# Attention's inner loop regrouped: tiles of four heads by 256 queries, three at a time

## The chip, the cores and the metric

The kernel runs on one core of a Trainium2 chip. The core has a matrix engine (TensorE, PE in the profile), a vector engine (VectorE, DVE), an activation engine (ScalarE, ACT), GpSimd (POOL) and SyncE (SP), which issues transfers. Matmuls write into PSUM, eight banks of 512 fp32 columns on each of 128 partitions; the other engines read from there. Each engine works through its own list of instructions in order and waits on semaphores. The metric is the device time of one execution in microseconds: the median over the runs of a kernel.

## The reference

Four layers, each added to its input after a layer norm: a long convolution (a state space model applied by FFT), an attention, the same convolution, the same attention. The change touches only the attentions. 2048 positions, width 640, 32 heads of 20 queries each; keys and values are shared by all heads.

```python
def _B_ref(x, wq, wk, wv, wo):
    B, S, D = x.shape          # 1, 2048, 640
    H = 32
    Dh = D // H                # 20
    q = (x @ wq).reshape(B, S, H, Dh).transpose(0, 2, 1, 3)
    k = x @ wk
    v = x @ wv
    scores = jnp.einsum("bhqd,bkd->bhqk", q, k) * (Dh ** -0.5)
    p = _softmax(scores, axis=-1)
    o = jnp.einsum("bhqk,bkd->bhqd", p, v)
    return o.transpose(0, 2, 1, 3).reshape(B, S, H * Dh) @ wo

x = A_u
x = x + _A_ref(_layernorm(x), ...)
x = x + _B_ref(_layernorm(x), ...)    # layer "b"
x = x + _A_ref(_layernorm(x), ...)
x = x + _B_ref(_layernorm(x), ...)    # layer "d"
return x
```

## The kernel before

`tile_layers` runs kgen, convolution "a", attention "b", convolution "c", attention "d". In an attention, `_attn` first projects queries and keys; queries go to DRAM, split into a high and a low part of fp32 (`qhd`, `qld`), the keys stay in `kt`, the values in `vt` (32 columns, of which one is all ones, so that the sums of the softmax come out beside the values). Then `main_loop` does the work that the change rewrites.

The loop's unit is a *step* (nb, hg, t): a block of 512 queries nb (four of them), a *head group* hg of four heads (eight of them), and 128 keys t (sixteen). A step has two halves, pr = 0 and 1, two heads each:

- `scores(step, pr)`: a *score pair*, two matmuls side by side on PE (62 rows each: 20 + 20 + 20 for the split of the query and key, and two for an offset), one for each head of the half, into a PSUM tile `sc` of 128 x 1024 (two banks; there are three such tiles, `ps2`), and one exponential on ACT from `sc` to the SBUF tile `pt`.
- `values(step)`: for each of the four heads one fp32 matmul of 512 columns into 32 partitions of the bank `po`, which sums over the sixteen t. The hardware runs an fp32 matmul as two passes, each with its own weight load; the four heads run side by side.
- `projection(nb, t)`: at t = 2, 5, 8, 11 and 13 one *product* out of a queue, if there is one: a piece of the output projection (128 queries x 320 columns, 128 rows of `wo`), four matmuls of 320 columns into the bank `py`; `add` then adds it to x on VectorE.
- `normalize(nb, hg)` after t = 15: VectorE copies `po` out, takes the reciprocal and multiplies; SP's queue moves the result into `ot`, which later products read.

The order on PE and ACT is that of the code (`manual_schedule`); for the other engines a scheduler places instructions. In the code, step s + 2's first half of scores comes ahead of step s's values, and its second half behind them and behind a product. `po` always lies in PSUM bank 0 of the two single ones (`ps1`), `py` in bank 1. So a new head group's first values wait until VectorE has copied the old sums out. A score pair waits until the exponential three pairs earlier has read its PSUM tile.

`load_q` brings a head group's queries from DRAM: two tiles `qp` of 128 x 512, one per half, 16 transfers in all, into six such buffers.

Of the kernel before, what the change touches and what calls it, by code (L numbers as in the profile page):

```python
# [21 lines left out]
P = 128  # L22
# [13 lines left out]
SCALE = 20.0**-0.5  # L36
# [159 lines left out]
class Net:  # L196
# [873 lines left out]
    def load_q(self, pool, nm, nb, hg):  # L1070

        nc = self.nc
        cols = slice(512 * nb, 512 * nb + 512)
        for pr in range(2):
            q = pool.tile([P, 512], F32R, tag="qp", bufs=6, name=f"qp{nm}{nb}{hg}{pr}")
            h = 4 * hg + 2 * pr
            for par in range(2):
                rows = slice(20 * (h + par), 20 * (h + par) + 20)
                for r, src in ((2, self.qhd), (22, self.qhd), (42, self.qld)):
                    nc.sync.dma_start(q[64 * par + r : 64 * par + r + 20].bitcast(F32), src[rows, cols])  # L1080
                nc.sync.dma_start(q[64 * par : 64 * par + 2].bitcast(F32), self.mxd[h + par, :, cols])  # L1081
            self.qps[nb, hg, pr] = q

    def _attn(self, ctx, nm, out):
        tc, nc, ins = self.tc, self.nc, self.ins
        ap = ctx.enter_context(tc.tile_pool(name=f"at{nm}", bufs=1, reuse_waits="tile"))
        kt = ap.tile([P, L], F32R, name="kt")
        vt = ap.tile([P, 16, 32], F32, name="vt")
# [153 lines left out]
        with tc.If(fv == 0):  # L1242
            self.row_max(kt, nm)
            for pr in range(2):
                for par in range(2):
                    nc.sync.dma_start(self.qps[0, 0, pr][64 * par : 64 * par + 2].bitcast(F32),
                                      self.mxd[2 * pr + par, :, 0:512])

        k0, k64 = keys(512, 3)
        nc.vector.tensor_scalar(k0, ones_(0, 3), off[0:1], None, ALU.mult)  # L1250
# [2 lines left out]
        mp = ctx.enter_context(tc.tile_pool(name=f"mn{nm}", bufs=1, reuse_waits="tile"))  # L1253
        self.main_loop(ap, mp, kt, vt, nm, out)

    def main_loop(self, ap, mp, kt, vt, nm, out):
# [10 lines left out]
        tc, nc, qps = self.tc, self.nc, self.qps  # L1267
        wo = mp.tile([P, 5, D], F32, name="wo")
# [4 lines left out]
        def late_loads(late):  # L1273
            nc.gpsimd.memset(wol, 0.0)
            for j in range(4):
                nc.gpsimd.dma_start(wol[32 * j : 32 * j + 20],
                                    self.ins["B_wo"][20 * (28 + j) : 20 * (29 + j)])
            if out is None:
                self.conv_weights(nc.gpsimd, late)
# [5 lines left out]
        def scores(step, pr):  # L1285
            nb, hg, t = step
            if t == 0 and pr == 0:
                if (nb, hg, 0) not in qps:
                    self.load_q(ap, nm, nb, hg)
            sc = self.ps2(f"sc{nm}{nb}{hg}{t}{pr}")  # L1290
            for par in range(2):
                rows = slice(64 * par, 64 * par + 62)
                nc.tensor.matmul(sc[:, 512 * par : 512 * par + 512],  # L1293
                                 kt[rows, 128 * t : 128 * t + 128], qps[nb, hg, pr][rows],
                                 start=True, stop=True)
            pt = mp.tile([P, 1024], F32, tag="pt", bufs=6, name=f"pt{nb}{hg}{t}{pr}")
            nc.scalar.activation(pt, sc, AF.Exp, scale=SCALE)  # L1297
            pts[step, pr] = pt

        def values(step):  # L1300
            nb, hg, t = step
            if t == 0:
                pos[nb, hg] = self.ps1(f"po{nm}{nb}{hg}", 0)
            po = pos[nb, hg]

            for j in (2, 3, 0, 1):
                nc.tensor.matmul(po[32 * j : 32 * j + 32], vt[:, t],  # L1307
                                 pts[step, j // 2][:, 512 * (j % 2) : 512 * (j % 2) + 512],
                                 start=(t == 0), stop=(t == 15))
            for pr in range(2):  # L1310
                del pts[step, pr]

        def chunk(nb, k):
            if (nb, k) not in ots:
                ots[nb, k] = mp.tile([P, 512], F32, tag=f"ot{k}", bufs=2, name=f"ot{nb}{k}")
                if (nb, k) == (3, 4):

                    nc.gpsimd.memset(ots[nb, k], 0.0)
            return ots[nb, k]

        def normalize(nb, hg):
            po = pos.pop((nb, hg))
            on = mp.tile([P, 512], F32, tag="on", bufs=2, name=f"on{nb}{hg}")
            nc.vector.tensor_copy(on, po)  # L1324
# [12 lines left out]
            for k in range(80 * hg // 128, 80 * (hg + 1) // 128):  # L1337
                later.extend((nb, k, u) for u in range(8))
# [25 lines left out]
        def product(py, o, w, u, m, start, stop):  # L1364
            i, half = u // 2, u % 2
            for j in range(0, P, m):
                nc.tensor.matmul(py[j : j + m], o[:, 128 * i + j : 128 * i + j + m],  # L1367
                                 w[:, 320 * half : 320 * half + 320], start=start, stop=stop)

        def projection(b, t):  # L1370

            if t == (8 if b < 3 else 5):
                queue.extend(later)
                later.clear()
            if t in (2, 5, 8, 11, 13) and queue:
                nb, k, u = queue.pop(0)
                py = self.ps1(f"py{nm}{nb}{k}{u}", 1)[:, 0:320]
                product(py, ots[nb, k], wo[:, k], u, 32, True, True)
                add(nb, u, py, k == 4)

        with tc.manual_schedule(engines={mybir.EngineType.PE, mybir.EngineType.Activation}):
            for step in steps[:2]:
                for pr in range(2):
                    scores(step, pr)
            for s, step in enumerate(steps):
                nb, hg, t = step
# [8 lines left out]
                if (nb, hg, t) == (0, 1, 0):  # L1395
                    late_loads(pts[steps[s + 2], 0])
# [8 lines left out]
            last.append(self.ps1(f"pl{nm}6", 1)[:, 0:320])  # L1405
            last.append(self.ps1(f"pl{nm}7", 0)[:, 0:320])
# [94 lines left out]
```

## Time and profile before

| what | value |
|---|---|
| median of 3 runs | 2982.32 us (2981.2 to 2982.5) |
| the profiled execution: its span, first to last instruction | 2978.7 us |
| attention loop of layer b, first exponential's start to the last one's | 720.4 to 1663.6 us |
| the same of layer d | 2015.0 to 2959.1 us |
| PE busy | 2771.9 us, 93% of the span |
| ACT busy | 2425.7 us, 81% |
| VectorE busy | 1374.8 us, 46% |

The trace holds one execution. The medians are of whole runs and stand 3.6 us above that span. Lines of the profile begin with the place in the code (L1293 is line 1293), the engine and the operation, then what is written from what; the names end in b or d for the layer. Numbers are microseconds, except the mean duration of one instruction, which is in nanoseconds. PE's matmuls overlap, so a matmul's own duration is longer than the time until the next one; the time between the starts of two groups of matmuls tells what the first one costs. A timeline row merges instructions of one kind that follow each other: its start, the time to the last one's end, and how many.

### The profile page before, as it was taken

To read this page: it belongs to the slowest core of one execution; us is meant where nothing else is said; L and a number is where in the kernel's file an instruction comes from. 1 tells how busy PE (TensorE), PEld (TensorE's weight loads), DVE (VectorE), ACT (ScalarE), POOL (GpSimd) and SP (SyncE) were. 2 spreads that over 40 slices of the span, in tenths; PEclk is the share of its full clock that TensorE was granted. 3 is DMA by queue.
4 is the path that set the end of the run, shared out by engine and by line. 5 is a ranking of instruction groups with operands and counts; after the bars stand their busy time and mean duration, and the time that the engine had idled before them with its cause. 6 is when DMAs were issued, how large, how long until landed. Compare 5 with 4: busy or idle time off the path is not lost. (4 is left out here: it accounts for less than half of the span.)

```text
span 2978.7 us, 52542 instructions
## 1 busy us (share of the span) xinstructions
PE 2771.9 (93%) x21712; PEld 1261.3 (42%) x21712; DVE 1374.8 (46%) x1800; ACT 2425.7 (81%) x2905; POOL 84.9 (3%) x140
## 2 busy tenths in 40 slices
PE   1776989998999999999999998899999999999999
PEld 0333978775223323233332687762233232332323
DVE  7999899942223232323232599731232323232323
ACT  5888243455999999999999634339999999999997
POOL 0000001100000000000000011000000000000000
PEclk9955999999999999999999999999999999999999
DMA  6113555533201010100000256231010101100100
GB/s 146 35 17 100 188 166 114 136 105 106 83 21 28 20 29 20 28 23 25 24 23 20 88 113 161 64 128 43 22 27 25 42 21 27 40 25 24 41 19 23
DMA packets 128240, 177.70 MB, mean 60 GB/s; under 512 B 59524, under 2 KB 84100, under 8 KB 124372
## 3 DMA queue, kind: packets, MB, share of 16 engines
q1 hardware_dynamic: 103832, 141.90, 16.2%
q0 software_dynamic: 21872, 30.69, 5.6%
q8 instruction: 175, 2.87, 0.4%
q10 hardware_dynamic: 2288, 1.64, 0.2%
q14 instruction: 73, 0.60, 0.1%
HBM read 95.22 MB, written 48.04 MB: 48 GB/s over the span
## 5 line engine op out<-in xcount | busy, mean ns | idle before, releaser
L1297 ACT ACTIVATE pt<-scd 128x1024 f32<-128x1024 f32 x1024 | 942.2, 1116 | 7.2 <-PE scd L1293 5.6
L1297 ACT ACTIVATE pt<-scb 128x1024 f32<-128x1024 f32 x1024 | 942.1, 1116 | 7.0 <-PE scb L1293 5.3
L1307 PE MATMUL pod<-pt,vt 128*32 128x512 f32 x4096 | 547.0, 606 | 4.4 <-DVE on L1324 0.3
L1307 PE MATMUL pob<-pt,vt 128*32 128x512 f32 x4096 | 546.4, 605 | 4.4 <-DVE on L1324 0.2
L1293 PE MATMUL scb<-qpb,kt 62*128 62x512 f32 x2048 | 385.7, 451 | 6.5 <-PEq L1242 6.1
L1293 PE MATMUL scd<-qpd,kt 62*128 62x512 f32 x2048 | 385.9, 451 | 5.9 <-PEq L1242 5.5
L1293 PEld LDWEIGHTS scb<-qpb,kt 62*128 62x128 f32 x2048 | 165.8, 184 | 402.2 <-ACT pt L1297 392.3
L1293 PEld LDWEIGHTS scd<-qpd,kt 62*128 62x128 f32 x2048 | 166.0, 185 | 401.8 <-ACT pt L1297 392.5
L1355 DVE TENSOR_TENSOR x<-pyd,x 128x320 f32<-128x320 f32 x146 | 71.8, 492 | 560.9 <-PE pyd L1367 560.9
L1355 DVE TENSOR_TENSOR x<-pyb,x 128x320 f32<-128x320 f32 x146 | 71.8, 492 | 547.4 <-PE pyb L1367 547.4
L1327 DVE RECIPROCAL rc<-rc 128x512 f32<-128x512 f32 x62 | 207.9, 3353 | 2.1
L1307 PEld LDWEIGHTS pod<-pt,vt 128*32 128x32 f32 x4096 | 80.6, 108 | 178.2 <-issue 160.2
L1307 PEld LDWEIGHTS pob<-pt,vt 128*32 128x32 f32 x4096 | 80.6, 108 | 177.7 <-issue 159.6
L1367 PE MATMUL pyb<-wo,ot 128*32 128x320 f32 x1168 | 105.3, 432 | 0.0
L1367 PE MATMUL pyd<-wo,ot 128*32 128x320 f32 x1168 | 105.3, 432 | 0.0
L654 PE MATMUL za<-xna,wf 128*128 128x256 f32 x384 | 87.1, 389 | 4.6 <-ACT xna L821 4.6
L654 PE MATMUL zc<-xnc,wf 128*128 128x256 f32 x384 | 85.7, 385 | 5.0 <-ACT xnc L821 5.0
L1324 DVE COPY on<-pod 128x512 f32<-128x512 f32 x31 | 21.4, 692 | 135.7 <-PE pod L1307 124.5
L445 PE MATMUL pe<-kg,tm 48*128 48x512 bf16 (+1 forms) x120 | 60.8, 610 | 23.8 <-ACT m L453 17.9
L1324 DVE COPY on<-pob 128x512 f32<-128x512 f32 x31 | 21.4, 692 | 132.3 <-PE pob L1307 119.8
L654 PEld LDWEIGHTS za<-xna,wf 128*128 128x128 f32 x384 | 74.4, 195 | 16.6 <-ACT xna L821 6.2
L654 PEld LDWEIGHTS zc<-xnc,wf 128*128 128x128 f32 x384 | 73.7, 193 | 16.3 <-ACT xnc L821 6.2
(372 smaller groups left out, 3182.3 us busy)
## 6 DMA issues: line engine op xcount, KB each, us to landing
Akh<-kh SPq DMA_DIRECT2D x10, 2048.0 KB
kh<-Ak SPq DMA_DIRECT2D x5, 2048.0 KB
qhd<-qh SPq DMA_DIRECT2D x40, 256.0 KB
qld<-ql SPq DMA_DIRECT2D x40, 256.0 KB
qpb<-qhd SPq DMA_DIRECT2D x256, 40.0 KB
qpd<-qhd SPq DMA_DIRECT2D x256, 40.0 KB
ot<-on SPq DMA_DIRECT2D x216, 40.0 KB
wi<-in_c_wi SPq DMA_DIRECT2D x16, 512.0 KB
```

The costliest lines, as they stand in the source:

```text
L445: nc.tensor.matmul(pe[:, 512 * h : 512 * h + 512], grp(tm, u, par, rows), kg[0:rows, col : col + 512], start=True, stop=True)
L654: nc.tensor.matmul(zv[:, :, c, kk], self.wf[:, t + 4 * h, j, c, kk], x, start=(n == 0), stop=(n == 3))
L1293: nc.tensor.matmul(sc[:, 512 * par : 512 * par + 512], kt[rows, 128 * t : 128 * t + 128], qps[nb, hg, pr][rows], start=True, stop=True)
L1297: nc.scalar.activation(pt, sc, AF.Exp, scale=SCALE)
L1307: nc.tensor.matmul(po[32 * j : 32 * j + 32], vt[:, t], pts[step, j // 2][:, 512 * (j % 2) : 512 * (j % 2) + 512], start=(t == 0), stop=(t ...
L1324: nc.vector.tensor_copy(on, po)
L1327: nc.vector.reciprocal(rc, rc)
L1355: nc.vector.tensor_tensor(xh, py, xh, ALU.add)
L1367: nc.tensor.matmul(py[j : j + m], o[:, 128 * i + j : 128 * i + j + m], w[:, 320 * half : 320 * half + 320], start=start, stop=stop)
```

## The change

The unit becomes a *tile*: four heads by 256 queries by 128 keys, 1024 of them a layer, in the order (nb, hg, f, t), where f is the half of the block's 512 queries. A tile has one score pair (again two matmuls of 512 columns: two heads of 256 queries in each) and one exponential of 128 x 1024; its values are four matmuls of 256 columns. PE's order is now made of groups of three: three score pairs, the values of three earlier tiles, and half a product (160 of 320 columns), if one is queued and no head group begins in or right behind the group. `po` lies in bank hg % 2, and `py` in the other one. Queries of a head group are one tile `qp` of 128 x 2 x 2 x 256, loaded by the same 16 transfers, each of them now in pieces of 256 columns; there are three such buffers, and seven of `pt` instead of six.

```diff
     def load_q(self, pool, nm, nb, hg):
-        cols = slice(512 * nb, 512 * nb + 512)
+        q = pool.tile([P, 2, 2, 256], F32R, tag="qp", bufs=3, name=f"qp{nm}{nb}{hg}")
         for pr in range(2):
-            q = pool.tile([P, 512], F32R, tag="qp", bufs=6, name=f"qp{nm}{nb}{hg}{pr}")
...
+                    nc.sync.dma_start(q[64 * par + r : 64 * par + r + 20, :, pr].bitcast(F32),
+                                      self.halves(src[20 * h : 20 * h + 20], nb))
+                self.load_rows(q, nb, h, par, pr)
...
-        steps = [(nb, hg, t) for nb in range(4) for hg in range(8) for t in range(16)]
+        tiles = [(nb, hg, f, t) for nb in range(4) for hg in range(8) for f in range(2) for t in range(16)]
...
+        def scores(i):
+            nb, hg, f, t = tiles[i]
+            if (nb, hg) not in qps:
+                self.load_q(ap, nm, nb, hg)
+            sc = self.ps2(f"sc{nm}{i}")
             for par in range(2):
                 rows = slice(64 * par, 64 * par + 62)
+                nc.tensor.matmul(sc[:, 512 * par : 512 * par + 512], kt[rows, 128 * t : 128 * t + 128],
+                                 qps[nb, hg][rows, f].rearrange("p a c -> p (a c)"), start=True, stop=True)
+            pt = pts[i] = mp.tile([P, 2, 2, 256], F32, tag="pt", bufs=7, name=f"pt{i}")
+            nc.scalar.activation(pt.rearrange("p a b c -> p (a b c)"), sc, AF.Exp, scale=SCALE)
+
+        def values(i):
+            nb, hg, f, t = tiles[i]
+            if (nb, hg) not in pos:
+                pos[nb, hg] = self.ps1(f"po{nm}{nb}{hg}", hg % 2)
+            po, pt = pos[nb, hg], pts.pop(i)
+
+            for j in range(4):
+                nc.tensor.matmul(po[32 * j : 32 * j + 32, 256 * f : 256 * f + 256], vt[:, t],
+                                 pt[:, j % 2, j // 2], start=(t == 0), stop=(t == 15))
...
+        def projection(hg, more):
+
+            if not part:
+                if not queue or not more:
+                    return
                 nb, k, u = queue.pop(0)
+                py = self.ps1(f"py{nm}{nb}{k}{u}", 1 - hg % 2)[:, 0:320]
+                part.extend((nb, k, u, py, c0) for c0 in (0, 160))
+            nb, k, u, py, c0 = part.pop(0)
+            product(py[:, c0 : c0 + 160], ots[nb, k], wo[:, k], u, 32, True, True, c0, 160)
+            if c0:
                 add(nb, u, py, k == 4)
...
-            for s, step in enumerate(steps):
-                nb, hg, t = step
-                if s + 2 < len(steps):
-                    scores(steps[s + 2], 0)
-                values(step)
-                projection(nb, t)
-                if s + 2 < len(steps):
-                    scores(steps[s + 2], 1)
-                if t == 15 and s + 1 < len(steps):
-                    normalize(nb, hg)
...
+            for i in range(3):
+                scores(i)
+            for k in range(0, n, 3):
+                group = range(k, min(k + 3, n))
+                for i in range(k + 3, min(k + 6, n)):
+                    scores(i)
...
+                for i in group:
+                    values(i)
+                    if i % 32 == 31 and i + 1 < n:
+                        normalize(*tiles[i][:2])
+                if k // 32 == (k + 2) // 32:
+                    if group[0] % 32 >= (15 if group[0] < n - 32 else 8):
+                        queue.extend(later)
+                        later.clear()
+                    projection(tiles[k][1], (k + 3) // 32 == (k + 5) // 32 == k // 32)
```

PE's order in the middle of a head group, layer b, before (sc are score pairs, po the sums of the values, py a product; a row ends with what the instruction waits for on another engine):

```order
L1307 MATMUL pob33_18422<-pt33121_18588,vt_4493 32x512 x2
L1307 MATMUL pob33_18422<-pt33120_18579,vt_4493 32x512 x2
L1293 MATMUL scb33141_18619<-qpb331_18370,kt_4492 128x512 [waits Activation_49]
L1293 MATMUL scb33141_18619<-qpb331_18370,kt_4492 128x512
L1293 MATMUL scb33150_18624<-qpb330_18361,kt_4492 128x512 [waits Activation_49]
L1293 MATMUL scb33150_18624<-qpb330_18361,kt_4492 128x512
L1307 MATMUL pob33_18422<-pt33131_18608,vt_4493 32x512 x2
L1307 MATMUL pob33_18422<-pt33130_18593,vt_4493 32x512 x2
L1367 MATMUL pyb305_18633<-wo_10732,ot30_17828 32x320 [waits DVE_49]
L1367 MATMUL pyb305_18633<-wo_10732,ot30_17828 32x320 x3
```

The same place of the changed program, in another head group of the same block:

```order
L1298 MATMUL scb780_19566<-qpb30_19410,kt_4492 128x512 [waits Activation_49]
L1298 MATMUL scb780_19566<-qpb30_19410,kt_4492 128x512
L1298 MATMUL scb781_19571<-qpb30_19410,kt_4492 128x512 [waits Activation_49]
L1298 MATMUL scb781_19571<-qpb30_19410,kt_4492 128x512
L1298 MATMUL scb782_19576<-qpb30_19410,kt_4492 128x512 [waits Activation_49]
L1298 MATMUL scb782_19576<-qpb30_19410,kt_4492 128x512
L1310 MATMUL pob30_19484<-pt777_19537,vt_4493 32x256 x4
L1310 MATMUL pob30_19484<-pt778_19542,vt_4493 32x256 x4
L1310 MATMUL pob30_19484<-pt779_19547,vt_4493 32x256 x4
L1368 MATMUL pyb232_19561<-wo_10731,ot23_18362 32x160 x4
```

Two pairs that waited for ACT stood between two steps' values; now three stand together, ahead of three tiles' values, and each of them waits for ACT on its own. A product of 320 columns now and then became 160 columns behind most groups: the whole order holds 290 of these halves a layer, where 146 products stood before.

The beginning of a head group's sums on PE, layer b, before (pob34 is the new sum):

```order
L1293 MATMUL scb3420_18702<-qpb340_18644,kt_4492 128x512 [waits Activation_49]
L1293 MATMUL scb3420_18702<-qpb340_18644,kt_4492 128x512
L1307 MATMUL pob34_18707<-pt3401_18674,vt_4493 32x512 [waits DVE_49]
L1307 MATMUL pob34_18707<-pt3401_18674,vt_4493 32x512
L1307 MATMUL pob34_18707<-pt3400_18665,vt_4493 32x512 x2
```

and in the changed program (pob36 is the old sum, pob37 the new one):

```order
L1310 MATMUL pob36_21703<-pt990_21980,vt_4493 32x256 x4
L1310 MATMUL pob36_21703<-pt991_21985,vt_4493 32x256 x4
L1310 MATMUL pob37_22062<-pt992_22007,vt_4493 32x256 [waits DVE_49]
L1310 MATMUL pob37_22062<-pt992_22007,vt_4493 32x256 x3
L1298 MATMUL scb996_22067<-qpb37_21987,kt_4492 128x512 [waits Activation_49]
```

Both wait for VectorE: before, for the copy of the old sum out of the same bank; now, for the addition of the last product, which was in the bank of the new sum. The old sum's last values and the new one's first stand in one group.

More of the change, by code (lines that the diff above doesn't have):

```diff
@@ L1245, in _attn @@
                 for par in range(2):
-                    nc.sync.dma_start(self.qps[0, 0, pr][64 * par : 64 * par + 2].bitcast(F32),
-                                      self.mxd[2 * pr + par, :, 0:512])
+                    self.load_rows(self.qps[0, 0], 0, 2 * pr + par, par, pr)
         k0, k64 = keys(512, 3)
@@ L1278, in late_loads @@
             if out is None:
-                self.conv_weights(nc.gpsimd, late)
-        steps = [(nb, hg, t) for nb in range(4) for hg in range(8) for t in range(16)]
+                self.conv_weights(nc.gpsimd, late.rearrange("p a b c -> p (a b c)"))
+        tiles = [(nb, hg, f, t) for nb in range(4) for hg in range(8) for f in range(2) for t in range(16)]
         pos, pts, ots = {}, {}, {}
         queue, later = [], []
-        def scores(step, pr):
-            nb, hg, t = step
[L1287 to L1290, printed above, removed]
+        def scores(i):
[3 more added lines that the diff above has]
+            sc = self.ps2(f"sc{nm}{i}")
@@ L1291, in scores @@
             for par in range(2):
                 rows = slice(64 * par, 64 * par + 62)
[L1293 to L1311, printed above, removed]
+                nc.tensor.matmul(sc[:, 512 * par : 512 * par + 512], kt[rows, 128 * t : 128 * t + 128],
+                                 qps[nb, hg][rows, f].rearrange("p a c -> p (a c)"), start=True, stop=True)
@@ L1362, in add, with product @@
                     eng.dma_start(self.rows(out)[jh][:, t], self.x[64 * jh : 64 * jh + 64, t])
-        def product(py, o, w, u, m, start, stop):
+        def product(py, o, w, u, m, start, stop, c0=0, n=320):
             i, half = u // 2, u % 2
+            c0 += 320 * half
             for j in range(0, P, m):
[L1367 to L1375, printed above, removed]
-                nb, k, u = queue.pop(0)
-                py = self.ps1(f"py{nm}{nb}{k}{u}", 1)[:, 0:320]
-                product(py, ots[nb, k], wo[:, k], u, 32, True, True)
+                nc.tensor.matmul(py[j : j + m], o[:, 128 * i + j : 128 * i + j + m], w[:, c0 : c0 + n],
+                                 start=start, stop=stop)
@@ L1379, in projection @@
+        part = []
+        def projection(hg, more):
+            if not part:
+                if not queue or not more:
+                    return
+                nb, k, u = queue.pop(0)
+                py = self.ps1(f"py{nm}{nb}{k}{u}", 1 - hg % 2)[:, 0:320]
[3 more added lines that the diff above has]
+            if c0:
                 add(nb, u, py, k == 4)
@@ L1381, in main_loop @@
         with tc.manual_schedule(engines={mybir.EngineType.PE, mybir.EngineType.Activation}):
-            for step in steps[:2]:
-                for pr in range(2):
-                    scores(step, pr)
-            for s, step in enumerate(steps):
-                nb, hg, t = step
-                if s + 2 < len(steps):
-                    scores(steps[s + 2], 0)
-                values(step)
-                projection(nb, t)
-                if s + 2 < len(steps):
-                    scores(steps[s + 2], 1)
-                if t == 15 and s + 1 < len(steps):
-                    normalize(nb, hg)
-                if (nb, hg, t) == (0, 1, 0):
-                    late_loads(pts[steps[s + 2], 0])
+            n = len(tiles)
@@ L1404, in main_loop @@
                 last += [tile_[:, 0:320], tile_[:, 512:832]]
-            last.append(self.ps1(f"pl{nm}6", 1)[:, 0:320])
-            last.append(self.ps1(f"pl{nm}7", 0)[:, 0:320])
+            last.append(self.ps1(f"pl{nm}6", 0)[:, 0:320])
+            last.append(self.ps1(f"pl{nm}7", 1)[:, 0:320])
             left = queue + later
```

14 lines of the change are left out of this document (9 added, 5 removed).

## The prediction

> **What bounds the kernel now.** The page first, for the shares and the costliest groups of instructions:
>
> ```profile
> span 2978.7 us, 52542 instructions
> ...
> PE 2771.9 (93%) x21712; PEld 1261.3 (42%) x21712; DVE 1374.8 (46%) x1800; ACT 2425.7 (81%) x2905; POOL 84.9 (3%) x140
> ...
> L1297 ACT ACTIVATE pt<-scd 128x1024 f32<-128x1024 f32 x1024 | 942.2, 1116 | 7.2 <-PE scd L1293 5.6
> ...
> L1307 PE MATMUL pod<-pt,vt 128*32 128x512 f32 x4096 | 547.0, 606 | 4.4 <-DVE on L1324 0.3
> ...
> L1293 PE MATMUL scd<-qpd,kt 62*128 62x512 f32 x2048 | 385.9, 451 | 5.9 <-PEq L1242 5.5
> ...
> L1355 DVE TENSOR_TENSOR x<-pyd,x 128x320 f32<-128x320 f32 x146 | 71.8, 492 | 560.9 <-PE pyd L1367 560.9
> ...
> L1367 PE MATMUL pyd<-wo,ot 128*32 128x320 f32 x1168 | 105.3, 432 | 0.0
> ```
>
> Two engines look full in the attention loop: PE, and ACT with its 1024 exponentials a layer. The instructions of the tile pt say how long each loop is:
>
> ```profile
> L1297 ACT ACTIVATE pt<-scb x1024: 1019/1096/1657, 720.4 to 1663.6; 128x1024 f32<-128x1024 f32 x171
> L1297 ACT ACTIVATE pt<-scd x1024: 1018/1097/1648, 2015.0 to 2959.1; 128x1024 f32<-128x1024 f32 x171
> ```
>
> From the first exponential's start to the last one's: 943.2 us in layer b, 944.1 in layer d, 1887.3 of the span's 2978.7. Which engine sets that? The timeline of one head group's time (29.5 us) in layer d, ACT first (the first row is one exponential in a window of its own), then PE, where a row begins when the first matmul of its kind is issued:
>
> ```profile
> 2428.12 1.02 ACT L1297 ACTIVATE pt<-scd 128x1024 f32<-128x1024 f32 x1
> ...
> 2428.12 28.52 ACT L1297 ACTIVATE pt<-scd 128x1024 f32<-128x1024 f32 x31
> ...
> 2457.62 1.02 ACT L1297 ACTIVATE pt<-scd 128x1024 f32<-128x1024 f32 x1
> ```
> ```profile
> 2425.38 0.73 PE L1293 MATMUL scd<-qpd,kt 62*128 62x512 f32 x4
> 2426.05 1.07 PE L1307 MATMUL pod<-pt,vt 128*32 128x512 f32 x8
> 2426.93 0.72 PE L1367 MATMUL pyd<-wo,ot 128*32 128x320 f32 x8
> 2427.58 0.73 PE L1293 MATMUL scd<-qpd,kt 62*128 62x512 f32 x4
> 2428.24 1.07 PE L1307 MATMUL pod<-pt,vt 128*32 128x512 f32 x8
> 2429.24 0.73 PE L1293 MATMUL scd<-qpd,kt 62*128 62x512 f32 x4
> 2429.90 1.06 PE L1307 MATMUL pod<-pt,vt 128*32 128x512 f32 x8
> 2430.90 0.74 PE L1293 MATMUL scd<-qpd,kt 62*128 62x512 f32 x4
> 2431.78 0.64 PE L1307 MATMUL pod<-pt,vt 128*32 128x512 f32 x4
> ```
>
> ACT: the first of 31 exponentials ends at 2428.12 + 1.02 = 2429.14, the last at 2428.12 + 28.52 = 2456.64, so one ends every 27.50 / 30 = 0.917 us. 1023 intervals at that rate are 938.1 us; the loops take 5.1 and 6.0 more. A head group's 32 exponentials take 32 x 0.917 = 29.34 of its 29.50 us (2428.12 to 2457.62), so about 0.16 is lost, once, where 2428.12 waits for its scores. **ACT bounds the loop, and no more than 11.1 us in all can be gained in it.**
>
> PE comes close. Two score pairs take 0.67 (2425.38 to 2426.05). A step's values take 0.88 when a projection product follows (2426.05 to 2426.93) and 1.00 when scores follow (2428.24 to 2429.24), so the change to scores costs 0.12. A product takes 0.65 - 0.12 = 0.53. A head group on PE is 16 x 1.67 + 4.56 x 0.53 = 29.1 (4.56 is 146 products over 32 groups).
>
> **The change part by part.** Two pairs, values of 512 columns and now and then a whole product became three pairs, three tiles' values of 256 columns and, nearly always, half a product. ACT still has 1024 exponentials of 128x1024 a layer: its floor stays.
>
> *PE's own time falls.* An fp32 product of 320 columns is two passes, 0.53 / 640 = about 0.84 ns a column; 512 columns by the same rate are 0.86 of the 0.88 above. So three tiles' values are 6 x 256 x 0.84 = 1.29, plus 0.02 for the first weight load and 0.12 for the change: 1.43. Half a product is 320 x 0.84 = 0.27. The third score pair costs what the second does: 0.67 less that of a pair alone, which the loop's end and one pair that waited show:
>
> ```profile
> 2958.58 0.49 PE L1293 MATMUL scd<-qpd,kt 62*128 62x512 f32 x2
> ...
> 2959.00 0.64 PE L1307 MATMUL pod<-pt,vt 128*32 128x512 f32 x4
> ```
> ```profile
> 2405.19 0.19 PEld L1293 LDWEIGHTS scd<-qpd,kt 62*128 62x128 f32 x2
> 2405.63 0.13 PEld L1307 LDWEIGHTS pod<-pt,vt 128*32 128x32 f32 x4 [0.24 <-issue]
> ```
>
> 0.42 and 0.44, so I take 0.43, and the third pair is 0.24. Three tiles: 0.91 + 1.43 + 0.27 = 2.61 us, where ACT needs 2.75. Before, the same work was 1.5 x 1.67 + 0.23 = 2.73. By sums alone the change helps. That isn't what decides.
>
> *The way from an exponential to the next scores becomes longer.* There are three score tiles in PSUM, so the scores of tile i wait for the exponential of tile i - 3. Call T the end of a group's third exponential. The third new pair waits for T, and behind it in PE's order stand three tiles' values, the half product and the next scores. Pieces that are still missing:
>
> ```profile
> 2015.05 1.02 ACT L1297 ACTIVATE pt<-scd 128x1024 f32<-128x1024 f32 x1 [4.31 <-PE scd L1293]
> ...
> 2016.12 0.29 PEld L1293 LDWEIGHTS scd<-qpd,kt 62*128 62x128 f32 x2 [0.99 <-ACT pt L1297]
> ```
>
> The exponential ends at 2016.07, the pair that waited for it begins at 2016.12: 0.05. From a pair's start (2427.58) to its exponential's (2428.12): 0.54; that one lasts 1.02. So after the change the first exponential of the next group but one ends at T + 0.05 + 0.43 + 1.43 + 0.27 + 0.54 + 1.02 = T + 3.74. ACT alone would end it four exponentials after T, at T + 3.67. It is late by 0.07. Six terms read to 0.01 leave some 0.03 to either side, 0.04 to 0.10; I take 0.08, since of the two lone pairs the one from the middle of the loop took the longer 0.44. Before, the same way had 1.00 + 0.53 in place of 1.43 + 0.27 and ended at T + 3.57, 0.10 early, which is why ACT lost time only where two products stand two steps apart.
>
> *How often.* Scores late in one group set back all later exponentials, so the next group, whose own way began earlier, is on time, and the one after is late again: every second group with a half product. The order has 290 halves a layer (before, 146 products). 145 x 0.08 = 11.6 us a layer. Groups without a half end at T + 3.47 and lose nothing.
>
> *The start.* There the granted clock is still low and PE takes twice as long:
>
> ```profile
> 2017.04 0.79 PE L1293 MATMUL scd<-qpd,kt 62*128 62x512 f32 x2
> 2017.77 1.93 PE L1307 MATMUL pod<-pt,vt 128*32 128x512 f32 x8
> 2019.63 0.79 PE L1293 MATMUL scd<-qpd,kt 62*128 62x512 f32 x2
> ...
> 2020.47 1.94 ACT L1297 ACTIVATE pt<-scd 128x1024 f32<-128x1024 f32 x2 [0.73 <-PE scd L1293]
> ```
>
> 0.73, 1.86 and 0.84. The first group's values then are 1.86 x 1.43 = 2.66, and T + 0.05 + 0.73 + 2.66 + 0.84 + 1.02 = T + 5.30 against 3.67: 1.6 lost.
>
> *The sum.* A loop: 938.1 + 11.6 + 1.6 = 951.3, against 943.2 and 944.1: 8.1 and 7.2 more, **15.3 us** in all. The span of 2978.7 becomes 2994.0; the median shown, 3.6 above that span, becomes **2998 us**.
>
> *Costed at nothing.* Sums in two banks: before, the first values of a head group waited for the sums' copy, 2430.90 to 2431.78, 0.88 where 0.67 is usual. At that place ACT lost nothing (the 31 exponentials above run through it), so what is freed is PE time. The products now share a bank with the last or next sums. At a head group's first values PE still waits for VectorE, but now for an addition of 0.49 us (the row of L1355), which was queued a group of PE's work earlier. Without this cover each of 32 boundaries a layer would cost up to 0.5, 32 us in all. The q loads become pieces of 256 columns; still 16 a head group, on SP's queue, each waiting for the tile freed three head groups earlier:
>
> ```profile
> L1080 SPq DMA_DIRECT2D qpd<-qhd x256: 272/324/1485, 1915.9 to 2873.1; - x128
> ```
>
> 16 x 0.32 is 5.2 us of issue in a head group of 29.5, and the last load begins at 2873.1, with the last head group's scores due some 56 us later (32 exponentials before 2959.1); twice that time would still fit. At the end one product more is left over (two passes of 320 columns, 0.54), and the last values are shorter by 512 columns (0.43): nothing.
>
> **Short passes.** An fp32 pass of 256 or 160 columns stands nowhere in the attention loop. Nearest rows: passes of 64 columns, and a convolution's of 256:
>
> ```profile
> 102.43 0.44 PE L482 MATMUL pk<-e1r,c 128*32 128x64 f32 x8
> 102.64 0.44 PE L482 MATMUL pk<-m,s 128*32 128x64 f32 x8
> ...
> L654 PE MATMUL za<-xna,wf 128*128 128x256 f32 x384 | 87.1, 389 | 4.6 <-ACT xna L821 4.6
> ```
>
> The first: eight matmuls (two passes of four) every 0.21, 0.107 a pass, so weights need no more than that, and a pass of 160 columns (0.134) covers it. The second: 87.1 / 384 = 0.227 each, with the pauses' pipeline tails in it, for 0.215 of columns. I take no surplus; above, 0.025 a pass, which the second score pair has (0.24 for 0.215).
> The Trainium skill, "TensorE: Matmul & The Clock Gate", section "Back-to-back issue gap", says that in a stream of weight loads and matmuls 128 columns take about 81 ns instead of 56, an extra of 25 ns. By that the eight short passes would add 0.2 to the way; the 64-column row, where 53 ns of columns take 107, has such an extra, the 256-column row hardly.
>
> **Rivals.** *ACT hides it all:* faster. Price: the way shrinks by 0.08 or more, from which point ACT never waits; loops 938.1 + 1.6 = 939.7, 7.9 less for both together: 2974. For it: PE's sums (2.61 of 2.75), and weight loads that PE runs ahead elsewhere. Against: at 2405.19 the weight load itself waited, so there is nothing to run ahead. *Short passes cost 0.025 more:* late by 0.28, 145 x 0.28 = 40.6 a layer, loops 980.3: 3056. The 64-column row speaks for it, the 256-column row against. *A wash:* late by 0.04, the lower end of the readings, and given back in part; loops 938.1 + 5.8 + 1.6 = 945.5, 2986, within what can be told from no change.
>
> **How the numbers follow.** The forecast 0.60, ACT hides it 0.18, a wash 0.14, short passes 0.08. The measurement tells 0.2%, about 6 us, from no change. Faster by more: 0.14 (four fifths of the first rival). Within: 0.18. Slower: 0.68. The forecast's own range, late by 0.05 to 0.12, is 2989 to 3010. The range that holds 8 of 10 reaches down to the first rival, 2973, and up to a surplus of 0.01 a pass (late 0.16), 3021.
>
> **What would show it.** Right: exponentials still end 0.917 us apart, but one of about six ends some 0.08 later, always the first of a group; from a group's first values to the next scores 1.43 without and 1.70 with half a product; a head group takes about 29.7 us. Wrong: no such delays and loops near 940 (PE's order isn't what ACT waits for), values above 1.50 (short passes cost more), delays of 0.3 and more at head group boundaries (the bank, or q).

## The result and the profile after

The changed kernel takes 3019.04 us (median of 4 runs, 3018.51 to 3020.89); the kernel before, run beside it, 2981.76 us (4 runs, 2980.76 to 2982.50). The ratio is 1.0129, with a 95% interval of 1.0115 to 1.0143. It is slower, as forecast, but by 37.3 us where the forecast's sum gave 15.3.

From the page of the changed kernel:

```profile
span 3019.1 us, 74426 instructions
...
PE 2791.9 (92%) x32212; PEld 1642.4 (54%) x32212; DVE 1368.7 (45%) x1798; ACT 2452.8 (81%) x2905; POOL 84.9 (3%) x140
...
L1301 ACT ACTIVATE pt<-scd 128x1024 f32<-128x1024 f32 x1024 | 955.6, 1037 | 12.6 <-DMA qpd<-mxd 4.6
...
L1310 PE MATMUL pod<-pt,vt 128*32 128x256 f32 x8192 | 514.2, 384 | 0.0
...
L1298 PE MATMUL scd<-qpd,kt 62*128 62x512 f32 x2048 | 407.2, 464 | 19.1 <-ACT pt L1301 6.7
...
L1368 PE MATMUL pyd<-wo,ot 128*32 128x160 f32 x2320 | 131.9, 299 | 0.0
```

The shares say almost nothing: PE and ACT are as full as before, 92% and 81%. Two rows have moved. Ahead of the scores (L1298) PE had stood idle for 5.9 us of a layer, and now does so for 19.1, the most of one cause, 6.7, for ACT: PE has time to spare, and the loop is longer all the same. And the mean exponential, 1116 ns before, is 1037 ns. That isn't a faster exponential. The records of two consecutive ones overlap, and one whose scores came just in time or late takes 1.02 us, the others more (up to 1.66 before the change). So a smaller mean says that ACT more often had nothing ready.

The instructions of the tile pt give the loops, first start to last start (the columns are least, middle and greatest duration in ns):

```profile
L1301 ACT ACTIVATE pt<-scb x1024: 1013/1027/1163, 720.9 to 1683.8; 128x1024 f32<-128x1024 f32 x171
L1301 ACT ACTIVATE pt<-scd x1024: 1016/1026/1159, 2036.4 to 2999.1; 128x1024 f32<-128x1024 f32 x171
```

962.9 and 962.7 us, where 943.2 and 944.1 stood: 38.3 us more in both. The profiled span grew by 40.4, so 2.1 of this execution lie outside the loops; the medians, 37.3 apart, leave nothing for that.

Now PE's timeline in the middle of a head group of layer d, and two exponentials, each in a window of its own:

```profile
2439.02 1.11 PE L1298 MATMUL scd<-qpd,kt 62*128 62x512 f32 x6
2440.06 1.50 PE L1310 MATMUL pod<-pt,vt 128*32 128x256 f32 x24
2441.38 0.46 PE L1368 MATMUL pyd<-wo,ot 128*32 128x160 f32 x8
2441.76 1.28 PE L1298 MATMUL scd<-qpd,kt 62*128 62x512 f32 x6
2442.97 1.50 PE L1310 MATMUL pod<-pt,vt 128*32 128x256 f32 x24
2444.29 0.46 PE L1368 MATMUL pyd<-wo,ot 128*32 128x160 f32 x8
2444.68 1.11 PE L1298 MATMUL scd<-qpd,kt 62*128 62x512 f32 x6
```
```profile
2438.55 1.03 ACT L1301 ACTIVATE pt<-scd 128x1024 f32<-128x1024 f32 x1
...
2439.63 1.02 ACT L1301 ACTIVATE pt<-scd 128x1024 f32<-128x1024 f32 x1
```

PE's groups begin at 2439.02, 2441.76 and 2444.68: 2.74 us, then 2.92. Two groups take 5.66, where ACT needs 6 x 0.917 = 5.50 for their six exponentials. So 0.16 is lost in every second group, and it is lost at one place: the group whose scores begin at 2439.02. The exponential before it ends at 2438.55 + 1.03 = 2439.58, its own first one at 2439.63 + 1.02 = 2440.65. That is 1.07 apart instead of 0.917, so 0.15 late. And it started 0.61 after its scores began (2439.02 to 2439.63), not 0.54.

I call an exponential *late* when it ends more than 0.917 + 0.04 us after the one before it. Counted over the ends of all 1024 exponentials of a layer (the first ten intervals apart, since PE's granted clock stands at 0.50 in layer d until 2022.1 us before and 2043.5 us after, and each further interval against 0.917; times in us):

| kernel, layer d | loop | lost in the first ten | lost later | late ones | mean lateness of these |
|---|---|---|---|---|---|
| before | 944.1 | 1.48 | 4.80 | 30 | 0.16 |
| the change | 962.7 | 1.68 | 23.17 | 155 | 0.15 |

That is what the forecast described (145 late ones, 1.6 at the start), but for the size of one event: 0.15, not 0.08. 155 x 0.15 = 23.2 is the whole of it.

### The profile page after: what moved, and what is told of

The parts are those of the page before. It is cut to its first block, busy times and chain, and to the rows that moved or that the text cites. A ratio compares the mean times of both kernels' runs of the same rounds, so it can differ in the third digit from the quotient of the medians.

```text
span 3019.1 us, 74426 instructions
## 1 busy us (share of the span) xinstructions
PE 2791.9 (92%) x32212; PEld 1642.4 (54%) x32212; DVE 1368.7 (45%) x1798; ACT 2452.8 (81%) x2905; POOL 84.9 (3%) x140
## 5 line engine op out<-in xcount | busy, mean ns | idle before, releaser
L1301 ACT ACTIVATE pt<-scb 128x1024 f32<-128x1024 f32 x1024 | 955.6, 1037 | 12.9 <-DMA qpb<-mxd 4.6
L1301 ACT ACTIVATE pt<-scd 128x1024 f32<-128x1024 f32 x1024 | 955.6, 1037 | 12.6 <-DMA qpd<-mxd 4.6
L1310 PE MATMUL pob<-pt,vt 128*32 128x256 f32 x8192 | 514.4, 384 | 0.0
L1310 PE MATMUL pod<-pt,vt 128*32 128x256 f32 x8192 | 514.2, 384 | 0.0
L1298 PE MATMUL scb<-qpb,kt 62*128 62x512 f32 x2048 | 407.2, 464 | 19.1 <-ACT pt L1301 6.3
L1298 PE MATMUL scd<-qpd,kt 62*128 62x512 f32 x2048 | 407.2, 464 | 19.1 <-ACT pt L1301 6.7
L1310 PEld LDWEIGHTS pob<-pt,vt 128*32 128x32 f32 x8192 | 231.6, 109 | 202.0 <-issue 83.0
L1310 PEld LDWEIGHTS pod<-pt,vt 128*32 128x32 f32 x8192 | 231.5, 109 | 201.6 <-issue 82.6
L1298 PEld LDWEIGHTS scb<-qpb,kt 62*128 62x128 f32 x2048 | 168.3, 185 | 244.3 <-ACT pt L1301 198.3
L1298 PEld LDWEIGHTS scd<-qpd,kt 62*128 62x128 f32 x2048 | 168.0, 185 | 244.8 <-ACT pt L1301 199.2
L1368 PE MATMUL pyd<-wo,ot 128*32 128x160 f32 x2320 | 131.9, 299 | 0.0
L1368 PE MATMUL pyb<-wo,ot 128*32 128x160 f32 x2320 | 131.9, 299 | 0.0
L1368 PEld LDWEIGHTS pyd<-wo,ot 128*32 128x32 f32 x2320 | 75.4, 110 | 49.8
L1368 PEld LDWEIGHTS pyb<-wo,ot 128*32 128x32 f32 x2320 | 75.4, 110 | 49.8
L445 PE MATMUL pe<-kg,tm 48*128 48x512 bf16 (+1 forms) x120 | 59.9, 602 | 23.7 <-ACT m L453 15.3
```

Source lines behind the costliest of these rows:

```text
L445: nc.tensor.matmul(pe[:, 512 * h : 512 * h + 512], grp(tm, u, par, rows), kg[0:rows, col : col + 512], start=True, stop=True)
L1298: nc.tensor.matmul(sc[:, 512 * par : 512 * par + 512], kt[rows, 128 * t : 128 * t + 128], qps[nb, hg][rows, f].rearrange("p a c -> p (a c) ...
L1301: nc.scalar.activation(pt.rearrange("p a b c -> p (a b c)"), sc, AF.Exp, scale=SCALE)
L1310: nc.tensor.matmul(po[32 * j : 32 * j + 32, 256 * f : 256 * f + 256], vt[:, t], pt[:, j % 2, j // 2], start=(t == 0), stop=(t == 15))
```

## Where the other 0.07 comes from

Everything that PE does on the way was as forecast. By the records of PE's starts in the changed program's layer d (medians), the third pair of a group starts 0.053 after its exponential's end (forecast 0.05), keeps PE for 0.432 (0.43), the three tiles' values for 1.433 where scores follow (1.43), and values with half a product 1.704 (1.70). What differs is behind PE: the scores' start to the exponential's start, 0.61 for 0.54. The order on ACT shows what an exponential waits for (the tile's number is left out of the names). Before:

```
L1297 ACTIVATE pt_31453<-scd_31450 128x1024 [waits PE_49]
L1297 ACTIVATE pt_31458<-scd_31455 128x1024 [waits PE_49,Activation_49]
L1297 ACTIVATE pt_31467<-scd_31464 128x1024 [waits PE_49]
L1297 ACTIVATE pt_31472<-scd_31469 128x1024 [waits PE_49,Activation_49]
```

and in the changed program:

```
L1301 ACTIVATE pt_35221<-scd_35218 128x1024 [waits PE_49,Activation_49]
L1301 ACTIVATE pt_35226<-scd_35223 128x1024 [waits PE_49,Activation_49]
L1301 ACTIVATE pt_35231<-scd_35228 128x1024 [waits PE_49,Activation_49]
L1301 ACTIVATE pt_35270<-scd_35267 128x1024 [waits PE_49,Activation_49]
```

PE_49 is the wait for the scores. Activation_49 is ACT's own counter: by the kernel's order, an earlier exponential that wrote the same `pt` buffer. That one is long past, but it is a second semaphore, and for each such pair the program has an instruction of its own on ACT's queue, ahead of the exponential: this one waits for PE, and the exponential behind it for ACT's counter. The instructions of the exponential's line, in the kernel before and in the changed one (count; least, middle and greatest ns):

```profile
L1297 ACTq EVENT_SEMAPHORE  x1029: 17/17/2632, 715.7 to 2957.2; - x172
```
```profile
L1301 ACTq EVENT_SEMAPHORE  x2046: 17/17/2387, 716.4 to 2999.0; - x186
```

For 2048 exponentials there were 1029 such instructions before, and there are 2046 now. The exponential from whose row the forecast took its 0.54 (2428.12 in the profile before) was one of those without. For the late ones of the changed kernel's layer d the trace gives the steps (medians): the wait instruction begins 0.040 us after the scores' end and takes 0.017, and the exponential starts 0.045 behind it, 0.10 after the scores in all. The late ones before, without such an instruction, started 0.042 after theirs.

## Experiments

**One wait for a group's first exponential.** `pt` gets three names in turn instead of one, with 3 + 2 + 2 buffers, so a buffer comes round again after nine or six tiles instead of seven. The order of all work stays, but on ACT a group's first exponential now waits for PE alone:

```
L1301 ACTIVATE pt_35221<-scd_35218 128x1024 [waits PE_49]
L1301 ACTIVATE pt_35226<-scd_35223 128x1024 [waits PE_49,Activation_49]
L1301 ACTIVATE pt_35231<-scd_35228 128x1024 [waits PE_49,Activation_49]
L1301 ACTIVATE pt_35270<-scd_35267 128x1024 [waits PE_49]
```

```diff
-            pt = pts[i] = mp.tile([P, 2, 2, 256], F32, tag="pt", bufs=7, name=f"pt{i}")
+            pt = pts[i] = mp.tile([P, 2, 2, 256], F32, tag=f"pt{i % 3}", bufs=2 if i % 3 else 3, name=f"pt{i}")
```

> The changed kernel, but the seven buffers of pt are split into three, two and two, by tile number modulo 3. Nothing else moves on PE. By the order on ACT the exponentials of each group's first tile then wait for PE alone, and no longer also for ACT's own old write into the buffer. Theory (the late exponential starts 0.105 us after its scores instead of 0.045, because a wait of its own instruction stands ahead of it): 145 x 0.06 = 8.7 us less in each loop, 954 us each, a median near 3001.5, and 0.045 from the scores' end to the late exponential's start. Rival (something slows the start of an exponential whatever it waits for, PE's writes into PSUM beside ACT's reads for one): no change, 3019.

Measured: 3001.49 us beside 2979.66 of the kernel before, ratio 1.0077 (1.0062 to 1.0093). The wait instructions of the exponential's line, its instructions, PE's timeline at a late group and that group's first exponential (alone in its window):

```profile
L1301 ACTq EVENT_SEMAPHORE  x1368: 17/17/2565, 715.4 to 2977.3; - x196
```
```profile
L1301 ACT ACTIVATE pt<-scb x1024: 1017/1025/1217, 719.7 to 1673.7; 128x1024 f32<-128x1024 f32 x171
L1301 ACT ACTIVATE pt<-scd x1024: 1017/1026/1215, 2026.2 to 2979.5; 128x1024 f32<-128x1024 f32 x171
```
```profile
2441.93 1.12 PE L1298 MATMUL scd<-qpd,kt 62*128 62x512 f32 x6
```
```profile
2442.47 1.02 ACT L1301 ACTIVATE pt<-scd 128x1024 f32<-128x1024 f32 x1
```

Two of three exponentials kept the instruction (2048 x 2 / 3 is 1365). From the scores' start to the exponential's it is 2442.47 - 2441.93 = 0.54 again. Again 155 exponentials a layer are late, but by 0.09, and the loops are 954.0 and 953.3 us, 8.9 and 9.4 less than in the changed kernel. The order of the work is the same and the 0.54 is back at the very place, so about half of what the change costs in the loop is this second wait, and the other half is the longer way that the forecast had.

**A whole product in every second group.** If the way from an exponential to the next scores sets the time, 320 columns at once must cost more than 160 twice; if PE's sum does, nothing changes.

```diff
-                part.extend((nb, k, u, py, c0) for c0 in (0, 160))
-            nb, k, u, py, c0 = part.pop(0)
-            product(py[:, c0 : c0 + 160], ots[nb, k], wo[:, k], u, 32, True, True, c0, 160)
-            if c0:
-                add(nb, u, py, k == 4)
+                part.append((nb, k, u, py))
+                return
+            nb, k, u, py = part.pop(0)
+            product(py, ots[nb, k], wo[:, k], u, 32, True, True)
+            add(nb, u, py, k == 4)
```

> The changed kernel, but a whole product of 320 columns behind every second group that has one, instead of half a product behind each. PE's work and the changes of kind stay the same, only half of it moves by one group. Theory (the way from a group's third exponential over values and product to the next scores sets the loop): the groups with a product are late by 0.15 + 0.27 = 0.42 where every second one was late by 0.15, so 145 x 0.27 = 39 us more a layer, loops near 1000, a median near 3095. Rival (PE's sum of work sets it, or the exponentials became slower as such): no change, 3019 within 3.

Measured: 3094.64 us, ratio 1.0390 (1.0374 to 1.0405).

```profile
L1301 ACT ACTIVATE pt<-scd x1024: 1016/1042/1163, 2069.5 to 3069.8; 128x1024 f32<-128x1024 f32 x171
```

The loops are 1000.4 and 1000.3 us: 144 late ones of 0.43 in each. The half product added to the way (0.27) is added to each event (0.15 to 0.43), while PE has the same columns to do in all. So in groups of three it is the way, and not PE's sum, that decides.

**Groups of two.** With two tiles' values instead of three, the same way has 1.00 for 1.43 in it.

```diff
-            for k in range(0, n, 3):
-                group = range(k, min(k + 3, n))
-                for i in range(k + 3, min(k + 6, n)):
+            for k in range(0, n, 2):
+                group = range(k, k + 2)
+                for i in range(k + 3, min(k + 5, n)):
                     scores(i)
...
+                if step in (1, 3, 4, 6, 7, 9, 10, 12, 13, 14):
+                    projection(tiles[k][1], step < 14)
```

> The changed kernel, but in groups of two: two score pairs, two tiles' values, and half a product in ten of a head group's sixteen groups; tiles of 256 queries, halves and two banks stay. Theory: the way is T + 0.05 + 0.43 + 1.00 + 0.27 + 0.60 + 1.02 = T + 3.37 against ACT's T + 3.67, so ACT never waits after the start: loops 938.1 + 1.5 = 939.6, a median near 2974, below the kernel before. Rival (PE's sum binds: 16 x 1.67 + 10 x 0.27 = 29.4 a head group with five products, ACT 29.34): loops 942 to 945, a median of 2979 to 2984, no better than before. Rival (tiles of 256 queries cost something else): above 2990.

Measured: 2977.10 us, ratio 0.9991 (0.9982 to 1.0000).

```profile
L1301 ACT ACTIVATE pt<-scb x1024: 1017/1144/1583, 720.4 to 1662.3; 128x1024 f32<-128x1024 f32 x171
L1301 ACT ACTIVATE pt<-scd x1024: 1017/1144/1590, 2014.3 to 2955.9; 128x1024 f32<-128x1024 f32 x171
```

941.9 and 941.6 us a loop. It falls between the two expectations: behind the start nearly all lateness is gone (1.6 us, 20 events of 0.07), but the start takes 2.6 and 2.2, more than in groups of three. The middle exponential of 1144 ns says that scores now are mostly early. The size of the group, then, is what turned the rest of the change into a loss: tiles of 256 queries, 290 halves a layer and two banks are all still in this kernel; beside the size only the places of the halves moved.

**All sums in bank 0 again.** Groups of three, but the new sums must wait for the copy of the old ones.

```diff
-                pos[nb, hg] = self.ps1(f"po{nm}{nb}{hg}", hg % 2)
+                pos[nb, hg] = self.ps1(f"po{nm}{nb}{hg}", 0)
...
-                py = self.ps1(f"py{nm}{nb}{k}{u}", 1 - hg % 2)[:, 0:320]
+                py = self.ps1(f"py{nm}{nb}{k}{u}", 1)[:, 0:320]
```

> The changed kernel, but all sums in one bank and all products in the other, as before the change. Theory (two banks were costed at nothing, for the cover of PE's other work; here that cover is gone, because the old sum's last values and the new one's first stand in one group): at 21 of 31 boundaries of a layer PE waits some 0.9 us for the copy, of which 0.12 are spare in these groups without a product: 21 x 0.78 = 16 us a layer, a median near 3052. Rival (the copy is hidden here too): 3019.

Measured: 3049.41 us, ratio 1.0235 (1.0219 to 1.0251): 30.4 more than the 3019.04 with two banks; the loops, 977.9 and 977.0, are longer by 15.0 and 14.3. PE's timeline at a boundary of head groups, and from the instructions of the tile pod who waited for it (us, times):

```profile
2480.62 0.64 PE L1310 MATMUL pod<-pt,vt 128*32 128x256 f32 x8
2482.07 1.07 PE L1310 MATMUL pod<-pt,vt 128*32 128x256 f32 x16 [0.81 <-DVE on L1324]
```
```profile
L1301 ACT ACTIVATE pt<-scb x1024: 1017/1026/1163, 720.4 to 1698.3; 128x1024 f32<-128x1024 f32 x171
L1301 ACT ACTIVATE pt<-scd x1024: 1015/1026/1163, 2051.0 to 3028.0; 128x1024 f32<-128x1024 f32 x171
...
  PE pod L1310: 17.1, 21
```

At 21 of 31 boundaries of layer d PE stands still for the copy, 0.81 each (17.1 / 21), since the new sums' first values follow right behind the old ones' last. The second bank is worth some 15 us a layer in this order. (VectorE and ACT are the only engines that read PSUM in this kernel, so the copy is VectorE's work.) With the second bank, PE's values wait for VectorE nowhere in the loop (0.0 idle in the row of L1310 above).

**Halves spread over the head group.** The some 20 late ones that were left in groups of two were all a head group's second exponential, which comes behind the three groups in a row with a half (12, 13, 14). My theory was that these three are their cause.

```diff
-                if step in (1, 3, 4, 6, 7, 9, 10, 12, 13, 14):
+                if step in (1, 2, 4, 5, 7, 8, 10, 11, 13, 14):
```

> The kernel in groups of two (e3), with the ten halves of a head group moved: two of every three of its sixteen groups, so that never three halves follow each other. Theory (where three halves follow, the way's reserve of 0.30 is used up and one exponential of a head group is late by some 0.07; the rest is the loop's start at a low clock): the late ones after the start vanish, 1.2 us less a loop, loops 938.1 + 2.3 = 940.4, 2 us less than e3 in all. Rival (they come with the head group's boundary, from the DMA waits of new queries or from the sums' copy): nothing changes.

Measured: 2977.17 us beside 2980.74, ratio 0.9987 (0.9978 to 0.9996); loops 942.3 and 942.0. The theory fell. The late ones did not vanish: there are 25 a layer, of 0.05, again a head group's second exponential, now in each of the last 25 head groups. PE's timeline over such a head group (16 groups) shows why:

```profile
2489.41 0.73 PE L1298 MATMUL scd<-qpd,kt 62*128 62x512 f32 x4
2490.08 1.07 PE L1310 MATMUL pod<-pt,vt 128*32 128x256 f32 x16
...
2518.81 0.74 PE L1298 MATMUL scd<-qpd,kt 62*128 62x512 f32 x4
```

2518.81 - 2489.41 = 29.40 us, without a wait on PE, where ACT's 32 exponentials need 29.34. So in groups of two PE's sum itself seemed to be the bound, by some 0.05 per head group; the last experiment below tells.

**The same with one wait for most exponentials.** Two names for `pt`, with three and four buffers.

```diff
-            pt = pts[i] = mp.tile([P, 2, 2, 256], F32, tag="pt", bufs=7, name=f"pt{i}")
+            pt = pts[i] = mp.tile([P, 2, 2, 256], F32, tag=f"pt{i % 2}", bufs=3 + i % 2, name=f"pt{i}")
```

> As e5, and the seven buffers of pt split into three and four by tile number modulo 2, so that by the order on ACT the exponentials of odd tiles, the first pair's of each group, wait for PE alone. Theory: after the start none is late, so the shorter wait is worth 0.06 us at the two late ones of the start alone, 0.2 us in all: the same as e5. Rival (the extra wait costs ACT time at every exponential): 512 x 0.06 = 31 us less a layer.

Measured: 2976.51 us, ratio 0.9986 (0.9977 to 0.9995), loops 941.5 and 941.3.

```profile
L1301 ACTq EVENT_SEMAPHORE  x1030: 17/17/2427, 715.8 to 2952.9; - x172
```
```profile
L1301 ACTq EVENT_SEMAPHORE  x2046: 17/17/2566, 717.0 to 2956.8; - x186
```

The first row is this kernel's, the second that of the kernel with the halves spread. A thousand wait instructions fewer are worth 0.8 and 0.7 us of loop, of which 0.6 and 0.4 are in its first ten intervals: nothing that can be told from the scatter. The rival, that each wait instruction takes time of ACT (31 us a layer), fell; a cost shows only where the exponential is late. This median is the lowest of the versions, 0.14% below the kernel before with an interval that leaves out 1, but it can't be told from that of the kernel with the halves spread (2977.17).

**Eight halves a head group.** If PE's sum is the bound in groups of two, it must cease to be with two halves fewer, 29.40 - 2 x 0.27 = 28.86. In each layer 27 more products are then left over. 25 of them, all of the last query block, are done at the layer's end. The other two, the third block's last, are left out, and with them what would follow for their 128 rows: in layer b the statistics for the next layer norm, in layer d the output. So this kernel doesn't compute the reference's result, and layer d works on what comes of it; layer b's loop stands ahead of all that.

```diff
-                if step in (1, 2, 4, 5, 7, 8, 10, 11, 13, 14):
-                    projection(tiles[k][1], step < 14)
+                if step in (1, 2, 4, 5, 8, 9, 11, 12):
+                    projection(tiles[k][1], step < 12)
```

> As e5, but eight halves in a head group instead of ten; what is not done in the loop, 27 products a layer, is done at the layer's end instead. e5's late exponentials did not vanish; each head group with ten halves has one, late by 0.046, and PE's work in such a group, 16 x 1.667 + 10 x 0.272 = 29.39 us, is 0.05 above ACT's 32 x 0.917 = 29.34. Theory (PE's sum): with eight halves PE has 28.85, and after the start no exponential is late any more; loops 938.1 plus the start's 2.3. Rival (head group boundaries: the new queries' DMA waits on PE, or the new sum's bank): one late by about 0.05 at each head group as in e5. The whole takes longer, 2 x 27 x 0.54 = 29 us of products at the ends, near 3004.

Measured, once: 3001.28 us beside 2981.51, as the work put off comes at the end (25 products a layer, not the 27 of the expectation), but the question is about the loops:

```profile
L1301 ACT ACTIVATE pt<-scb x1024: 1018/1216/1583, 721.0 to 1661.0; 128x1024 f32<-128x1024 f32 x171
L1301 ACT ACTIVATE pt<-scd x1024: 1018/1216/1591, 2026.5 to 2965.4; 128x1024 f32<-128x1024 f32 x171
```

940.0 and 938.9 us. Behind the first ten no exponential is late, and the floor of 938.1 is reached but for the start (2.4 and 1.3). The middle record of 1216 ns is the longest of all: here the scores wait for ACT. Layer b's loop alone shows it. PE's sum was the cause of what groups of two still lost.

## Why the prediction was right and wrong

**What bounds the kernel:** right. ACT's exponentials are the floor, 0.917 us each, and the last kernel reaches it behind its start.

**PE's own time falls:** right to 0.01 us for the values (1.433), half a product (0.271) and a lone pair (0.432). The 0.91 for three pairs almost never appears, since the third one waits for ACT (1.04 in the timeline above). It was right, too, that the sum doesn't decide in groups of three. Whole products instead of halves, which leave PE's columns as they are, moved the time by over 75 us. In groups of two, where the way is shorter, it does decide, by some 0.05 a head group.

**The way from an exponential to the next scores:** this is where the step failed, in one term. The way's mechanism, its place (a group's first exponential) and five of its six terms hold. The term 0.54, from a pair's start to its exponential's, was taken from an exponential that waits for one semaphore, while after the change all of them wait for two. It is 0.61 there. With the measured pieces the sum is 0.053 + 0.432 + 1.704 + 0.61 + 1.02 = 3.82, late by 0.15 against 3.67, and 0.15 was measured. With the second wait taken away at that place the late ones were late by 0.09, and the loops 954.0 and 953.3 where 951.3 was forecast. The forecast's bounds for it, 0.04 to 0.10, were the reading error of the rows; that a row might not be of the same kind of instruction was not in them.

**How often:** nearly right, every second group, 155 late ones for the forecast's 145; where the ten more come from was not looked into. So 11.6 us a layer became 23.2, 23.1 more in both layers together; the forecast's loops were short by 23.0 (1925.6 for 1902.6), its difference of the medians by 22.0.

**The start:** 1.6 was forecast; 1.96 (b) and 1.68 (d) were measured, where 0.55 and 1.48 stood before. ACT's timeline in layer d shows it in one place, behind the sixth exponential:

```profile
2036.44 5.61 ACT L1301 ACTIVATE pt<-scd 128x1024 f32<-128x1024 f32 x6 [4.57 <-DMA qpd<-mxd]
2043.63 1.02 ACT L1301 ACTIVATE pt<-scd 128x1024 f32<-128x1024 f32 x1 [1.58 <-PE scd L1298]
```

The seventh waits 1.58 for its scores, which stand behind the first group's values. The loss goes along with the length of the low clock, which wasn't forecast: in layer b the granted clock stood at 0.50 for the loop's first 8.5 us, before the change only for 4.6; in layer d for 7.1 in both. In groups of two with ten halves the first ten intervals lost 2.1 to 2.8; no run tells what makes that start longer.

**Costed at nothing:** right. That the kernel with one bank lost 30.4 us, where the forecast's price for a lost cover was 32, is chance: 0.81 for the copy at 21 boundaries a layer is not 0.5 for the addition at 32. With two banks PE's values wait for nothing, and of ACT's waits for the queries' transfers the 4.6 us in the page's row are the 4.57 ahead of the loop.

**Short passes:** right to take no surplus. 1.433 less 0.02 and 0.12 over six passes is 0.215 for 256 columns, and (1.704 - 1.433) / 2 = 0.136 for 160: both what 0.84 ns a column give, to 0.002. The Trainium skill, "TensorE: Matmul & The Clock Gate", section "Back-to-back issue gap", gives about 81 ns instead of 56 for a matmul of 128 columns in a stream of weight loads and matmuls; these passes of 160 and 256 columns, each with a weight load, don't show such an extra of 25 ns.

**Rivals.** *ACT hides it all* did not come true for the change, but its condition, a way shorter than four exponentials, is what groups of two meet: 941.6 to 941.9 a loop, for the 939.7 that the rival gave. *Short passes* and *a wash* fell: 1.433 for the values, and a loss well beyond what can be told from no change.

## What to carry to other kernels

Where two engines are both nearly full, the sums of their work give only a lower bound. It was reached here in groups of two, and missed in groups of three, where a longer way decided. So besides the sums, follow the way from one engine's result round through the other and back, over as many units as there are buffers between them, and compare it with the time of these units on the slower engine. Each thing put into one uninterrupted stretch of that way counted in full as long as the way was the longer of the two: here small groups won over large ones, and half a product behind each group over a whole one behind every second, with the same total. And take a latency only from a row whose instruction has the same waits as the one to be predicted: here the order of the waiting engine showed the difference, which the order of the engine whose work was moved could not.

## What was not expected of the hardware

A second semaphore to wait for, though it had been set long before, made a late exponential start 0.10 us after its scores' end instead of 0.04 (0.61 for 0.54 from the scores' start), by a wait instruction whose own record is 17 ns. Taken away at the place where it mattered, in one exponential of three, it gave 9 us a layer; taken away from half of all exponentials in a kernel whose scores are early, nothing that can be told from the scatter. Why the kernel before had it on only every other exponential, and which rule puts it there, was not looked into.
